# A scan and an ELU layer on one core: B and C of the later blocks turned by VectorE instead of TensorE, and the sums of the first layer's quarters joined

## The chip, the core and the metric

The kernel runs on one core of one Trainium2 chip. The metric is the device time of a whole execution in microseconds. The kernel before was run three times: 364.29, 364.76 and 364.16, median 364.29. One further execution was profiled; its span, from the first to the last instruction, is 362.9.

## The reference

There are two layers. The first is a chunked state-space scan over x (4 batches, 8 heads, 768 tokens, 32 wide) with decays a and with B and C (16 wide). The second takes the scan's output as 3072 tokens of 256 and computes ELU between two matrix products, 256 to 2048 and back.

```python
for c in range(nc):
    CB = np.einsum('bhin,bhjn->bhij', Cc, Bc)
    M = CB * L                                  # L: causal decays
    y_intra = np.einsum('bhij,bhjd->bhid', M, xc)
    y_inter = np.einsum('bhin,bhnd->bhid', Cc, state) * decay_to_i
    y[:, :, sl] = y_intra + y_inter
    state = decay_full * state + np.sum(Bx, axis=2)
h = x @ w_in
g = np.where(h > 0.0, h, np.exp(np.minimum(h, 0.0)) - 1.0)
out = g @ w_out
```

All of it is float32 (the weights come as 64-bit words that the kernel turns into float32 itself).

## The kernel before, in words

**Tiles.** The tokens are cut into 12 blocks of 256 (`NP`), all 8 heads in one. `place(n)` says which batch and which third a block is. A block has two halves of 128 tokens (`u`), and each of these two chunks of 64 (`v`).

**The scan of a block.** `load_bc` (line 106) brings B and C with the tokens on the partitions. `scaled` (line 359, on POOL) multiplies B by the decays. `turn` (line 368) brings B and C to the form with 8 heads x 16 states on the partitions: four TensorE transposes (line 374) into two PSUM tiles, a copy of B by ScalarE (line 378, `bt`), a masked C by VectorE (line 381, `ctm`). `turn_exp` (line 385) multiplies C by the decays `ec` (line 389, `cts`); `spread_exp` (line 340) fetches `ec` with one DMA per head. `scores` (line 450) multiplies masked C with B on TensorE, `weigh` (465) applies the decays, `sums` and `states` (480, 496) carry the state on, `across` and `inside` (522, 542) give the scan's output transposed in PSUM, which is copied to `yT`.

**The two matrix products.** Blocks 0 to 3 use plain products (`l1`, `l2`, lines 577 and 700) with ELU between them (`elu`, 598: exponential on ScalarE, then one VectorE instruction, line 605). From block 4 on, pairs of blocks n, n+1 are multiplied by a scheme with seven products where plain blocks take eight. For the first product each of 8 pieces i of a pair takes seven part products of 256 columns (line 655; each is two TensorE instructions in the profile) in two PSUM tiles c1 and c2 of one bank each. They are issued in three groups: `front` (three products, and a copy of the first by ScalarE, line 665), `mid` (two), `back` (two). Between them VectorE makes five sums of 256 columns: two in `front_sums` (673, 674), one in `mid` (682), two in `back` (689, 690). Then c1 and c2 go on the list `lag` and through ELU: `begin_elu` issues ScalarE's Relu (596), `elu` the rest. For the second product, `second(n)` (line 736) is a generator that gives out 56 small steps of products (line 759), with sums on VectorE and POOL (line 750, and `sub` at 723, `sum_t1` at 725, `sum_t2` at 729).

**The order of the work** is written out by hand: each engine does its instructions in the order in which the program issues them. The loop at line 1051 takes the pairs n = 4, 6, 8, 10, one stage each; a stage has 16 half steps k, two for each piece i = k // 2. An even half step does `front`, `front_sums`, the rest of an ELU, and four steps of the second product of the pair before (`l2s`). An odd one does `mid`, two steps, `back`, one step, the rest of an ELU and the start of the next. `scan_ahead` (967) puts the scan of the next pair between them: in stage n the loads and decays at k = 0 to 2, the turns at k = 5 and 7, `scores` at k = 9, and at i = 5 a version with `weigh`, `sums` and `states`. The stages n = 2 and n = 3 (line 1011) take single blocks.

**Buffers.** PSUM has 8 tiles of one bank: 7 in the pool `p_a`, given out in turn, and 1 in `p_o`. A new tile waits until the one seven before it has been read for the last time.

## Time and profile before

| engine | busy, us | share of the span | instructions |
|---|---|---|---|
| TensorE, matmuls (PE) | 354.3 | 98% | 3978 |
| TensorE, weight loads (PEld) | 316.9 | 87% | 3978 |
| VectorE (DVE) | 242.2 | 67% | 547 |
| ScalarE (ACT) | 200.7 | 55% | 499 |
| GpSimd (POOL) | 227.1 | 63% | 366 |

The matrix engine's clock is granted in full over the whole span, and the DMA engines are busy mostly in the first fifth. The costliest group of instructions is line 759 (the second product): 640 + 320 + 160 matmuls at 275 ns each. That is the time from the start of one to its end; they overlap, and in a stretch without waits one starts every 110 ns. Those of line 655 (256 columns) take 383 ns and start every 217 ns. VectorE's five sums per piece, of 32 pieces, are 13.5, 13.6, 13.8, 13.7 and 13.8 us. How to read a row of the timeline: start and length in us, engine, line, operation, output and inputs with shapes, and in brackets how long the engine had been idle before and what ended that.

### The profile page before, as it was taken

Reading aid. Unit: us, or ns where it says so; the run is one execution under the profiler, and the core shown is the slowest. Engines: PE = TensorE matmul, PEld = TensorE weight load, DVE = VectorE, ACT = ScalarE, POOL = GpSimd, SP = SyncE. Lnnn points to the kernel's source line nnn. Section 1 sums busy time; section 2 is a strip of 40 time slices with the busy share of each in tenths; the row PEclk is TensorE's granted clock in tenths of the full one; section 3 lists DMA queues with packets and bytes.
Section 4 is the critical chain, followed back from the end, with each engine's and each line's share of the span. In section 5 each row is a group of like instructions: output and inputs, shape, how many; then the busy total and the mean of one; then the engine's idle time right before and its main releaser. Section 6 shows DMA issues by size and latency. Waiting matters only on the chain.

```text
span 362.9 us, 10146 instructions
## 1 busy us (share of the span) xinstructions
PE 354.3 (98%) x3978; PEld 316.9 (87%) x3978; DVE 242.2 (67%) x547; ACT 200.7 (55%) x499; POOL 227.1 (63%) x366
## 2 busy tenths in 40 slices
PE   8899999999999999999999999999999999999996
PEld 5578778888888998898999998999989999999995
DVE  4989887972697668784567684666685666666212
ACT  4858969767435567635485735386735352534100
POOL 4454443663567896679457578567587555456893
PEclk9999999999999999999999999999999999999999
DMA  8877995563050560053530045540000100000001
GB/s 155 203 203 147 240 308 141 66 116 63 3 116 19 65 85 12 4 115 48 96 65 2 3 95 68 93 72 0 3 2 4 58 2 0 3 0 32 29 2 58
DMA packets 96239, 25.33 MB, mean 70 GB/s; under 512 B 77312, under 2 KB 92096, under 8 KB 96192
## 3 DMA queue, kind: packets, MB, share of 16 engines
q1 hardware_dynamic: 94016, 24.49, 33.0%
q8 instruction: 31, 0.51, 0.6%
q10 hardware_dynamic: 2176, 0.20, 0.4%
q14 instruction: 16, 0.13, 0.1%
HBM read 21.33 MB, written 3.34 MB: 68 GB/s over the span
## 4 chain that ended last, share of the span: by engine, by line
PE 81%; DVE 7%; ACT 3%; DMA 3%; SPq 2%; issue 2%; POOL 1%; ACTq 0%; DVEq 0%
PE ps_o L759 32%; PE ps_h L655 25%; PE ps_h L583 10%; PE ps_o L707 8%; SPq L112 2%; PE ps_g L459 1%; DMA w<-in_moe_w_in_dram 1%; DVE g L605 1%; PE ps_y L553 1%; ACT e L596 1%; PE ps_st L489 1%; ACT e L603 1%; DMA flat<-F 1%; DVE mag L183 1%; PE ps_y L534 1%
## 5 line engine op out<-in xcount | busy, mean ns | idle before, releaser
L596 ACT ACTIVATE e<-ps_h 128x512 f32<-128x512 f32 x96 | 56.5, 588 | 93.1 <-DVE ps_h L689 71.2
L605 DVE SCALAR_TENSOR_TENSOR g<-e,ps_h 128x512 f32<-128x512 f32 x96 | 65.3, 681 | 39.2 <-ACT e L603 35.8
L759 PEld LDWEIGHTS ps_o<-w_out,g 128*128 128x128 f32 x640 | 80.3, 192 | 3.3 <-issue 0.5
L759 PE MATMUL ps_o<-w_out,g 128*128 128x128 f32 x640 | 81.4, 275 | 0.0
L727 POOL TENSOR_TENSOR g<-g 128x256 f32<-128x256 f32 x34 | 24.8, 729 | 67.1 <-DVE g L605 67.1
L583 PE MATMUL ps_h<-yT,w_in 128*128 128x256 f32 x256 | 60.6, 383 | 2.5 <-POOL w_in L200 1.8
L603 ACT ACTIVATE e<-e 128x512 f32<-128x512 f32 x96 | 60.9, 634 | 2.2
L583 PEld LDWEIGHTS ps_h<-yT,w_in 128*128 128x128 f32 x256 | 47.8, 190 | 10.6 <-POOL w_in L200 2.8
L759 PE MATMUL ps_o<-w_sum,g 128*128 128x128 f32 x320 | 43.0, 275 | 0.0
L759 PEld LDWEIGHTS ps_o<-w_sum,g 128*128 128x128 f32 x320 | 41.1, 192 | 1.4
L439 ACT ACTIVATE L<-L,ncum 128x64 f32<-128x64 f32 x160 | 41.0, 338 | 0.0
L655 PE MATMUL ps_h<-y_sum,w_in 128*128 128x256 f32 x128 | 38.6, 383 | 0.7 <-DVE ps_h L682 0.7
L655 PE MATMUL ps_h<-y_sum,w_sum 128*128 128x256 f32 x128 | 38.5, 382 | 0.5 <-DVE g L605 0.5
L655 PE MATMUL ps_h<-yT,w_in 128*128 128x256 f32 x128 | 38.8, 385 | 0.0
L444 POOL TENSOR_SCALAR_AFFINE_SELECT L<-L 64x512 f32<-64x512 f32 x40 | 27.3, 682 | 13.1 <-ACT L L439 11.8
L707 PE MATMUL ps_o<-w_out,g 128*128 128x256 f32 x128 | 30.8, 383 | 0.0
L655 PEld LDWEIGHTS ps_h<-y_sum,w_sum 128*128 128x128 f32 x128 | 23.9, 190 | 5.3 <-DVE g L605 1.3
L723 POOL TENSOR_TENSOR g<-t,g 128x256 f32<-128x256 f32 x40 | 27.9, 729 | 0.8 <-PE ps_o L759 0.8
L723 POOL TENSOR_TENSOR t<-g 128x256 f32<-128x256 f32 x40 | 28.1, 736 | 0.2
L723 POOL TENSOR_TENSOR g<-g,t 128x256 f32<-128x256 f32 x40 | 27.9, 730 | 0.2
L707 PEld LDWEIGHTS ps_o<-w_out,g 128*128 128x128 f32 x128 | 23.7, 190 | 3.4 <-POOL L L444 0.2
L689 DVE TENSOR_TENSOR ps_h<-ps_h,u_sum 128x256 f32<-128x256 f32 x32 | 13.7, 429 | 18.3 <-PE ps_h L655 18.3
(109 smaller groups left out, 538.3 us busy)
## 6 DMA issues: line engine op xcount, KB each, us to landing
L<-flat SPq DMA_DIRECT2D x20, 256.0 KB, 5.3
w<-in_moe_w_in_dram SPq DMA_DIRECT2D x8, 512.0 KB, 5.2
w<-in_moe_w_out_dram SPq DMA_DIRECT2D x8, 512.0 KB, 6.1
xr<-in_x_dram SPq DMA_DIRECT2D x24, 128.0 KB, 3.4
out_dram<-c_sum SPq DMA_DIRECT2D x10, 256.0 KB, 2.1
bc<-in_B_dram SPq DMA_DIRECT2D x24, 64.0 KB, 4.4
bc<-in_C_dram SPq DMA_DIRECT2D x22, 64.0 KB, 3.4
ec<-flat_exp SPq DMA_DIRECT2D x72, 16.0 KB, 1.7
```

The costliest lines, as they stand in the source:

```text
L439: nc.scalar.activation(L[:, h, u], L[:, h, u], ACT.Exp, bias=ncum[:, u, row:row + 1])
L444: nc.gpsimd.affine_select(out=part, in_=part, pattern=[[0, 4], [0, 2], [1, Q]], compare_op=ALU.is_ge, fill=0.0, base=0, channel_multiplier=-1)
L583: nc.tensor.matmul(out=ps[:, j], lhsT=w_in[:, k, m * P:(m + 1) * P], rhs=yT[n // 2][:, k, n % 2].rearrange("p u i -> p (u i)"), start=(k = ...
L596: nc.scalar.activation(begun[0], lag[0][2], ACT.Relu, scale=-1.0)
L603: nc.scalar.activation(e, e, ACT.Exp, scale=-1.0)
L605: nc.vector.scalar_tensor_tensor(out=g_of[n, i], in0=e, scalar=1.0, in1=ps, op0=ALU.subtract, op1=ALU.max)
L655: nc.tensor.matmul(out=out, lhsT=lhsT, rhs=rhs, start=first, stop=True, skip_group_check=True)
L689: nc.vector.tensor_tensor(out=c1[:, 1], in0=c1[:, 1], in1=u[:, 0], op=ALU.add)
L707: nc.tensor.matmul(out=o_of[n][:, ts], lhsT=g_of[n, j][:, m % 2, ts * P:(ts + 1) * P], rhs=w_out[:, m], start=(m == 0 and ts == 0), stop=( ...
L723: nc.gpsimd.tensor_tensor(out=out, in0=in0, in1=in1, op=ALU.subtract)
L727: eng.tensor_tensor(out=b12, in0=b12, in1=g_of[n, i][:, 0], op=ALU.subtract)
L759: nc.tensor.matmul(out=ps[:, ts], lhsT=b[:, ts * P:(ts + 1) * P], rhs=a[:, i], start=(i == chunk[0] and ts == 0), stop=(i == chunk[-1]), s ...
```

## The change

From block 6 on B and C no longer pass through TensorE and PSUM. `load_bc` fetches B twice: once with the tokens on the partitions, for `scaled`, and B and C once more in an order (4 heads x 32 groups of 8 tokens on the partitions) in which VectorE's transposes of 32x32 squares give the wanted form. `turn_square` issues one such VectorE instruction for B and one for C; `mask_heads` and `turn_exp` follow, now from SBUF. `turn_step` deals these four parts of two blocks out over the odd half steps 1, 3, 5, 7 of a stage, an early place between `mid` and `back` and a late one after `back`; block 6's first three come in stage n = 3. The loads are issued half a stage sooner. `spread_exp` becomes one DMA.

In the first product the part products change their places: c2 takes the two that `front` leaves open and both of `back`, c1 those of `mid`'s sum. `front_sums` is then one sum over both halves of c2, `mid` has one of 256 columns, and `back` one over both halves of c2. c1 is complete after `mid` and goes on the list there. Because the quarters lie elsewhere, `second` finds them through `quarters`. In the loop `begin_elu` now follows `mid`, and `next_elu`, `begin_elu` follow `back` ahead of the one step; at i = 5 the steps are 4, 1, 2 for 3, 2, 2. In the beginning `w_sum(0)` is done in quarters. Some pools have fewer buffers (`sc`, `cts`, `ob`), and `bt` becomes a tile for B and C.

```diff
@@ load_bc
+        if n > 5:
+            st[n]["b"] = raw.tile([P, 2, NH, N], F32, tag="b", name="b_tok", bufs=2)
+            for u in range(2):
...
+                nc.sync.dma_start(
+                    out=st[n]["b"][:, u], in_=B[b, :, sl, :].rearrange("h s n -> s h n"))
...
+            for k, src in enumerate((B, C)):
+                for m in range(2):
+                    nc.sync.dma_start(
+                        out=squares[:, k, m],
+                        in_=src[b, m:NH:2, g * BLK:(g + 1) * BLK, :].rearrange(
+                            "q (c t) n -> q c (t n)", t=8))
+            return
@@ spread_exp
-        for h in range(NH):
-            row = rows_of(n).start + NG * h
-            nc.sync.dma_start(
-                out=ec[N * h:N * (h + 1)].rearrange("n u i -> n (u i)"),
-                in_=flat_exp[row:row + 1].to_broadcast([N, BLK]))
+        nc.sync.dma_start(
+            out=ec.rearrange("p u i -> p (u i)"),
+            in_=flat_exp[rows_of(n)].unsqueeze(1).to_broadcast([NH, N, BLK]))
@@ after turn
+    def turn_square(n, k):
...
+        nc.vector.transpose(
+            out=s["squares"][:, k].rearrange("p u i -> p (u i)").rearrange("p (c t) -> p t c", t=8),
+            in_=s["bc"].rearrange("p k u h n -> p k (u h n)").rearrange(
+                "p k (m t n) -> p k t m n", m=2, n=N)[:, k])
...
+    def turn_part(n, part):
+        if part < 2:
+            turn_square(n, 1 - part)
+        elif part == 2:
+            mask_heads(n)
+        else:
+            turn_exp(n)
@@ front, front_sums, mid, back
-        copy = conv.tile([P, BLK], F32, tag="sgn", name="p_copy")
-        nc.scalar.copy(out=copy, in_=c1[:, 0])
-        part_product(c2[:, 1], s_in[0][:, i], t[:, 1], True)
-        part_product(c2[:, 0], a21[:, i], t[:, 0])
+        u = conv.tile([P, 3, BLK], F32, tag="mag", name="u_sum")
+        nc.scalar.copy(out=u[:, 0], in_=c1[:, 0])
+        part_product(c2[:, 0], s_in[0][:, i], t[:, 1], True)
+        part_product(c2[:, 1], a21[:, i], t[:, 0])
...
-        nc.vector.tensor_tensor(out=u[:, 0], in0=c2[:, 1], in1=copy, op=ALU.add)
-        nc.vector.tensor_tensor(out=u[:, 1], in0=c2[:, 0], in1=u[:, 0], op=ALU.add)
+        nc.vector.tensor_tensor(
+            out=u[:, 1:3], in0=c2, in1=u[:, 0].unsqueeze(1).to_broadcast([P, 2, BLK]), op=ALU.add)
...
-        part_product(c1[:, 1], s_in[1][:, i], y_sums[n][:, 2])
-        nc.vector.tensor_tensor(out=c2[:, 1], in0=c1[:, 1], in1=u[:, 1], op=ALU.add)
+        part_product(c2[:, 0], s_in[1][:, i], y_sums[n][:, 2])
+        nc.vector.tensor_tensor(out=c1[:, 1], in0=c2[:, 0], in1=u[:, 2], op=ALU.add)
+        lag.append((n, i, c1))
...
-        part_product(c1[:, 1], a22[:, i], y_sums[n][:, 3])
-        part_product(c2[:, 0], s_in[2][:, i], b22)
-        nc.vector.tensor_tensor(out=c1[:, 1], in0=c1[:, 1], in1=u[:, 0], op=ALU.add)
-        nc.vector.tensor_tensor(out=c2[:, 0], in0=c2[:, 0], in1=u[:, 0], op=ALU.add)
-        lag.append((n, i, c1))
+        part_product(c2[:, 0], a22[:, i], y_sums[n][:, 3])
+        part_product(c2[:, 1], s_in[2][:, i], b22)
+        nc.vector.tensor_tensor(out=c2, in0=c2, in1=u[:, 0:2], op=ALU.add)
         lag.append((n + 1, i, c2))
@@ scan_ahead
-                load_bc(m + i)
+                if m == 4:
+                    load_bc(m + i)
...
-            if i in (5, 7):
+            if m == 4 and i in (5, 7):
...
+        if n % 2 == 1 and i in (1, 3) and n + 3 + i // 2 < NP:
+            load_bc(n + 3 + i // 2)
+        if n == 3 and i > 3 and i < 7:
+            turn_part(6, i - 4)
@@ after scan_ahead
+    def turn_step(n, k, late):
...
+        if m == 6:
+            steps = [(7, 0), (7, 1), (7, 2), (6, 3)]
+            if not late:
+                turn_part(*steps[k // 2])
+            elif k == 7:
+                turn_part(7, 3)
+        else:
+            at = k // 2 * 2 + late
+            turn_part(*[(m, 0), (m, 1), (m, 2), (m + 1, 0), (m + 1, 1), (m + 1, 2), (m, 3), (m + 1, 3)][at])
@@ the loop over pairs, odd half steps
                 mid(n, i)
...
+                begin_elu()
+                turn_step(n, k, False)
                 l2s(2)
                 back(n, i)
-
+                next_elu()
+                begin_elu()
+                turn_step(n, k, True)
...
                 l2s(1)
-                next_elu()
-                begin_elu()
```

## The prediction

> **What bounds the kernel now.** I read the page's first part first, then the busy time of the engines by stretches, then the chain of work that ended last, then single stretches of the timeline.

> ```profile
> PE 354.3 (98%) x3978; PEld 316.9 (87%) x3978; DVE 242.2 (67%) x547; ACT 200.7 (55%) x499; POOL 227.1 (63%) x366
> ...
> 110.00:167.00 57.00, 56.33 (x813) 51.47 (x815) 40.85 (x99) 31.25 (x82) 45.00 (x75) 1.00 0.34 53
> 167.00:224.00 57.00, 56.54 (x700) 51.73 (x684) 37.88 (x89) 33.43 (x88) 39.19 (x63) 1.00 0.32 54
> 224.00:277.00 53.00, 52.95 (x636) 49.04 (x637) 34.94 (x81) 32.16 (x86) 35.03 (x56) 1.00 0.17 30
> ```

> The stretches read: window, its length, then PE, PEld, DVE, ACT, POOL busy with counts. From 44 us on the chain of work is the matrix engine almost without a break, so time is saved by taking PE work out or PE waits out, and by nothing else. DVE is free for about a third of each stretch. The PE work that the change removes is in these rows (the line's own answer, and the chain in order of time with start, length, what):

> ```profile
> L374 PE MATMUL ps_tb<-ident,bc x24: 272/273/327, 6.7 to 254.9; 128*128 128x128 f32 x24
> L374 PE MATMUL ps_tc<-ident,bc x24: 272/273/273, 6.9 to 255.1; 128*128 128x128 f32 x24
> ```
> ```profile
> 139.07 0.68 DVE ctm L381
> 139.76 0.33 DVE cts L389
> 140.09 0.34 DVE u_sum L673
> 140.43 0.02 issue
> 140.45 0.42 DVE u_sum L674
> 140.88 0.06 DVE g L605
> 140.94 0.45 issue
> 141.39 0.42 DVE c_sum L750
> 141.80 0.35 DVE ps_h L682
> 142.16 0.04 issue
> 142.20 1.13 PE ps_h L655 x4
> 143.33 0.44 PE ps_o L759 x4
> 143.77 0.22 PE ps_tb L374 x2
> 143.99 0.22 PE ps_tc L374 x2
> ```

> A turn is four PE instructions, two times 0.22 us: 0.44 us per block. The 273 ns of one is latency, overlapped with the next. The same stretch shows the largest PE stall: from 139 to 142 us the chain leaves PE and runs through DVE, where mask (ctm), scaling (cts) and sums stand in one queue ahead of L682. The other stalls of this phase are at the first front of stages six and eight:

> ```profile
> 168.16 0.30 PEld L655 LDWEIGHTS ps_h<-y_sum,w_sum 128*128 128x128 f32 x2 [0.60 <-DVE g L605]
> 223.82 0.30 PEld L655 LDWEIGHTS ps_h<-y_sum,w_sum 128*128 128x128 f32 x2 [0.67 <-DVE g L605]
> ```

> There a PSUM tile is not free until ELU of the pair before has been done. Measured from start to start of the matmuls (217 ns apart when nothing waits), PE loses at these places: 0.15 + 0.83 us at 139 to 142, 0.36 at 168, 0.43 at 224, and 0.10 more on the first matmul after a wait, seven times: 2.5 us in all.

> [...] L674 with 256 takes 424 ns, L605 with 512 takes 681.

> **The change part by part.**

> *Turns on DVE.* Blocks 6 to 11 lose 4 PE transposes each: 6 x 0.44 = **2.64 us off PE**, all on the path. They also lose an ACT copy (358 ns) and two PSUM tiles each. DVE gains 12 squares of 128x256. Unknown; nearest price 424 ns[...]. I take 0.42. The mask then reads SBUF where it read PSUM (682 ns; taken the same), and the scaling 0.41 as before. Per stage DVE gains 4 x 0.42 = 1.7 us. It hides in the gaps shown here (start, length, instruction, idle before):

> ```profile
> 237.00 0.69 DVE L605 SCALAR_TENSOR_TENSOR g<-e,ps_h 128x512 f32<-128x512 f32 x1 [0.89 <-ACT e L603]
> ...
> 240.06 0.43 DVE L682 TENSOR_TENSOR ps_h<-ps_h,u_sum 128x256 f32<-128x256 f32 x1 [0.51 <-PE ps_h L655]
> ...
> 241.39 0.43 DVE L689 TENSOR_TENSOR ps_h<-ps_h,u_sum 128x256 f32<-128x256 f32 x1 [0.89 <-PE ps_h L655]
> ```

> The early piece stands between L682's sum and the joined last sum, where DVE waits 0.89 us for PE; because the joined sum waits for both quarters (0.43 more) the gap is 1.3 us. The late piece stands behind ELU's subtraction and ahead of the joined front sum.

> *Joined sums.* Five DVE sums of 421 to 430 ns (2.13 us) become one of 512, one of 256, one of 512: 0.69 + 0.43 + 0.69 = 1.81. 32 x 0.32 = 10 us off DVE, more than the 12 x 0.42 = 5 us of squares. On PE: nothing directly. One wait is new: the middle's second product (c2[0]) now waits for the joined front sum. Behind it on PE stand the two second-product steps, the back and everything after. In before I compared the end of L674 with the start of that product: DVE is ahead by 0.80 us in 13 of 32 pieces, by 0.1 to 0.6 in the rest but five; the joined sum ends 0.15 earlier than L674. Of those five one is the place at 139 to 142 that loses its cause, three are level within 0.03 (first piece of stages six and eight, last piece of the last), one has 2.8. So new waits: about 0, taken in the next paragraph for the stage heads.

> *Order of ELU.* c1 is whole after the middle, so ACT's Relu starts half a step earlier and c1's PSUM tile comes free earlier. At 164 to 168 us in before, Relu waited until 166.12 for two back sums that stood behind a c_sum waiting for POOL; now it starts about 1.5 us sooner, more than the 0.36 and 0.43 lost there. But the copy of P1 there stands behind six yT copies on ACT (168 to 170): joined sum no sooner than 170.08 + 0.37 + 0.69 = 171.14 if ACT is not earlier, and PE, 0.47 sooner, wants it at 170.87. So of some 0.6 us at each head (0.36 or 0.43, and two refills) I count 0.35, as ACT is partly earlier. **0.7 us.** At 139 to 142 the mask, one scaling, the bt copies and the PSUM tiles leave; of 1.18 us I count **1.1**. The last 0.10 (332.67) I leave.

> *Stage three.* Two squares and a mask (1.5 us) are added to DVE at steps 4 to 6, where it also makes weight sums. DVE is idle 3.25 us before 118.90, and the tiles behind are needed two steps later: nothing.

> *DMA.* load_bc of blocks 6 to 11 goes from 4 issues to 6 (about 0.6 us each on SP) and moves one half stage forward, past spread_cum and the loads of x. SP is idle there (no issue from 135 to 156 us), and the buffer it waits for is read last by POOL's scaled (88.83 to 90.06 in stage three). spread_exp goes from 8 issues (3.8 to 5.5 us of SP) to one. Its readers come ten us later: nothing.

> *First weight piece.* w_sum in halves: two POOL adds of about 0.49 us for one of 0.84. The first l1 can start 0.3 earlier, DVE beside it may slow. That phase ends on DMA landings (the chain goes flat, SP, w until 35.14): 0, with 0.3 either way.

> **Sum.** 2.64 + 1.1 + 0.7 = 4.4 us off the span of 362.9: 358.5. The runs are 364.16 to 364.76, median 364.29, some 1.4 above the profiled span; taken off the median: **359.9**.

> **Rivals.**

> 1. *Only the transposes pay.* The waits come back at the new place, the middle behind the joined sum, because ACT's copy and POOL's c_sum set DVE's times and not DVE's own load. For it: the three level pieces, and DVE c_sum waits for POOL (10.5 us in 6 waits). Against: 27 pieces with slack. 364.3 - 2.6 = 361.7, with half of it given back 363.0. If new waits eat all 2.6, 364.3: no change.

> 2. *Slower: a square is too long for its gap.* The late piece has 0.42 us plus the rest to the middle's product: joined sum at 237.46 to 238.15 against 239.43 in the stretch shown, 1.2 us. So PE waits once late squares pass 1.6 us, or an early one 1.3. In stages six and eight k=1 holds two squares, k=3 one late, k=5 one early. At 2.6 us each PE loses 1.3 + 2.2 - 1.2 = 2.3 at k=1, 1.0 at k=3, 0.4 at k=5: 3.6 a stage, 7.2 in all, 364.3 - 4.4 + 7.2 = 367.1. Even at about 2.2 us. For it: 32-byte steps on the output, on which the trace is silent.[...]

> 3. *More is gained.* All 2.5 us of waits and 0.3 at the start: 364.3 - 2.6 - 2.5 - 0.3 = 358.9, or 358.2 if the first pieces after the scores also flow better.

> **Numbers.** Forecast (359.2 to 361) 0.57; only the transposes (361 to 363.3) 0.20; more gained (below 359.2) 0.10; no change 0.04; slower 0.09. A measurement of this kernel tells 0.2%, 0.73 us, from no change. Faster by that 0.87, same 0.04, slower 0.09. The range 358.4 to 363.2 leaves out the slower and no-change cases and the edge of the third.

> **What would show it.** Right: L374 with 24 PE matmuls instead of 48; DVE squares near 0.42 us; front and last sums near 0.69; no PE stall over 0.3 us at the place of 139 to 142; PE busy time down 2.6 us with the span. Wrong: L655's weight loads waiting for the front sums in many pieces; squares over 1.3 us; c_sum on DVE waiting longer for POOL than 10.5 us; or a start that ends later than 44 us. What would upset the whole: a PE order that is no longer gapless because ACT, not DVE, ends last at each stage's head.

## The result, and the profile after

The changed kernel takes 363.01 us in the median of 9 runs (360.79 to 364.12), beside 365.23 us (9 runs) for the kernel before. The ratio is 0.9945, 95% interval 0.9924 to 0.9966: **2.0 us faster** (1.2 to 2.8; the two medians lie 2.2 apart), where 4.4 us were forecast. A second series of 22 runs gave 0.9952 (0.9932 to 0.9972). The profiled span is 362.1 us; before it was 362.9.

The page's busy times and its row of granted clock, kernel after:

```profile
PE 352.8 (97%) x3954; PEld 315.5 (87%) x3954; DVE 240.4 (66%) x495; ACT 200.8 (55%) x493; POOL 232.0 (64%) x368
...
PEclk9999999999999999999999999999998999999999
```

PE has 24 matmuls less, but only 1.5 us less busy time, and its share fell from 98% to 97%. The new thing is the single 8 in the clock row: slice 31 of 40, 271.6 to 280.6 us. Windows around it, kernel after (window, its length, busy of PE, PEld, DVE, ACT, POOL with counts, clock, DMA share, GB/s):

```profile
255.00:267.00 12.00, 12.00 (x178) 10.55 (x177) 8.60 (x22) 6.16 (x16) 9.52 (x16) 1.00 0.01 1
267.00:269.00 2.00, 1.99 (x103) 1.67 (x102) 1.90 (x5) 0.56 (x2) 0.98 (x4) 1.00 0.03 8
269.00:271.30 2.30, 0.48 (x46) 0.32 (x25) 0.15 (x1) 0.37 (x1) 2.22 (x4) 1.00 0.00 0
271.30:275.50 4.20, 4.20 (x84) 3.77 (x84) 0.00 (x0) 1.84 (x5) 3.00 (x5) 0.59 0.01 4
275.50:285.00 9.50, 9.50 (x65) 8.91 (x64) 5.86 (x12) 4.35 (x9) 4.46 (x7) 1.00 0.09 29
```

In the third window PE works 0.48 of 2.30 us, and DVE, ACT and DMA are next to idle as well. Only POOL is busy (2.22 us), with sums of the second product, and the trace shows no wait of PE for it. In the fourth the clock is 0.59. The timeline of PE's matmuls there, after and then before (start, length, instruction, count, idle before):

```profile
267.52 1.24 PE L576 MATMUL ps_y<-cts,Sx 32*64 32x64 f32 x64
268.69 0.79 PE L595 MATMUL ps_y<-M,xr 64*32 64x64 f32 x56
271.30 1.07 PE L595 MATMUL ps_y<-M,xr 64*32 64x64 f32 x72 [1.81 <-issue]
272.30 2.07 PE L807 MATMUL ps_o<-w_sum,g 128*128 128x128 f32 x8
274.17 1.06 PE L697 MATMUL ps_h<-yT,w_in 128*128 128x256 f32 x2
```
```profile
272.28 0.91 PE L534 MATMUL ps_y<-cts,Sx 32*64 32x64 f32 x64
273.12 1.51 PE L553 MATMUL ps_y<-M,xr 64*32 64x64 f32 x128
274.56 1.16 PE L759 MATMUL ps_o<-w_sum,g 128*128 128x128 f32 x8
```

This is the last call of `across` and `inside`, 192 small products back to back; I call such a stretch a **dense part**. Before, the 128 products of `inside` run in 1.51 us. After, PE stops in their middle, after 56, and the view names no releaser ("issue"). From 272.0 to 275.4 us matmuls are then twice as far apart, 427 ns instead of 217 at 256 columns: eight of L807 take 2.07 us instead of 1.16. In the trace's record the clock is one half for 3.41 us there, from 0.7 us after the end of a standstill of 2.0 us (start to start, 269.27 to 271.30 us).

To see what the rest of the change brought, I cut each profiled span at the first product of the first dense part and of the last one (in the timeline, the first L576; L534 before):

```
kernel        to first dense   first to last dense   last dense to end   span
before             111.57            160.72                90.62         362.9
turns_only         110.58            158.21                90.90         359.7
sums_only          112.02            159.44                90.74         362.2
after              110.92            156.60                94.58         362.1
after_again        111.99            156.77                94.14         362.9
```

The middle column holds the turns and most of the sums, and there the change takes off 160.72 - 156.60 = **4.1 us** (4.0 in the second profile), close to the 4.4 of the forecast. Then 94.58 - 90.62 = **4.0 us** are given back (3.5 in the second), in a stretch where only the joined sums are new, and `sums_only` takes 90.74 there. In the median of all runs the loss is less: both profiled executions had a mean granted clock of 0.993, while 21 of the change's 31 runs had 0.998 or more (and 18 of 49 runs of the kernel before had 0.995 or less, so a stretch at half clock is nothing new).

### The profile page after: what moved, and what is told of

Its sections match the earlier page's. It is cut to its first block, busy times and chain, and to the rows that moved or that the text cites. A ratio compares the mean times of both kernels' runs of the same rounds, so it can differ in the third digit from the quotient of the medians.

```text
span 362.1 us, 9921 instructions
## 1 busy us (share of the span) xinstructions
PE 352.8 (97%) x3954; PEld 315.5 (87%) x3954; DVE 240.4 (66%) x495; ACT 200.8 (55%) x493; POOL 232.0 (64%) x368
## 4 chain that ended last, share of the span: by engine, by line
PE 88%; POOL 5%; DVE 4%; issue 1%; ACT 1%; POOLq 0%; DVEq 0%
PE ps_o L807 32%; PE ps_h L697 25%; PE ps_h L625 14%; PE ps_o L746 8%; PE ps_y L595 2%; PE ps_g L501 2%; POOL g L762 2%; PE ps_y L576 1%; PE ps_st L531 1%; PE ps_idle L232 1%; POOL g L774 1%; DVE mag L207 1%; DVE mag L200 1%; POOL w_sum L673 1%; DVE M L510 1%
## 5 line engine op out<-in xcount | busy, mean ns | idle before, releaser
L807 PEld LDWEIGHTS ps_o<-w_out,g 128*128 128x128 f32 x640 | 80.3, 192 | 3.3 <-issue 0.5
L807 PE MATMUL ps_o<-w_out,g 128*128 128x128 f32 x640 | 81.4, 275 | 0.0
L807 PE MATMUL ps_o<-w_sum,g 128*128 128x128 f32 x320 | 43.9, 279 | 0.0
L807 PEld LDWEIGHTS ps_o<-w_sum,g 128*128 128x128 f32 x320 | 41.9, 195 | 1.5 <-PE ps_y L595 0.2
L730 DVE TENSOR_TENSOR ps_h<-ps_h,u_sum 128x512 f32<-128x512 f32 x32 | 22.3, 698 | 23.6 <-PE ps_h L697 23.5
L486 POOL TENSOR_SCALAR_AFFINE_SELECT L<-L 64x512 f32<-64x512 f32 x40 | 28.1, 702 | 13.0 <-ACT L L481 11.7
L722 DVE TENSOR_TENSOR ps_h<-ps_h,u_sum 128x256 f32<-128x256 f32 x32 | 13.8, 431 | 30.5 <-PE ps_h L697 30.1
L714 DVE TENSOR_TENSOR u_sum<-ps_h,u_sum 128x512 f32<-128x512 f32 x32 | 22.0, 687 | 13.3 <-PE ps_h L697 8.0
L762 POOL TENSOR_TENSOR t<-g 128x256 f32<-128x256 f32 x40 | 29.4, 767 | 0.3
L762 POOL TENSOR_TENSOR g<-g,t 128x256 f32<-128x256 f32 x40 | 28.7, 750 | 0.3
```

The source lines that it names most:

```text
L486: nc.gpsimd.affine_select(out=part, in_=part, pattern=[[0, 4], [0, 2], [1, Q]], compare_op=ALU.is_ge, fill=0.0, base=0, channel_multiplier=-1)
L730: nc.vector.tensor_tensor(out=c2, in0=c2, in1=u[:, 0:2], op=ALU.add)
L762: nc.gpsimd.tensor_tensor(out=out, in0=in0, in1=in1, op=ALU.subtract)
L807: nc.tensor.matmul(out=ps[:, ts], lhsT=b[:, ts * P:(ts + 1) * P], rhs=a[:, i], start=(i == chunk[0] and ts == 0), stop=(i == chunk[-1]), s ...
```

## The experiments

Two theories. **L** (supply of instructions): the trace has a DMA queue that carries instructions. It brings PE's in blocks of 16 KB, 31 of them in a run. The traces hold 8056 instructions of PE before and 8011 after (matmuls, weight loads and some hundred others), so a block is about 256 of them; the places of the standstills will show the number. Where one block ends and the next begins I call a **border**. A dense part of 384 instructions in 2.4 us eats such a block faster than the queue, which needs about 2.4 us from the start of a fetch to the first use (268.93 to 271.30 us in the profile after), can bring the next. In the profile after, PE has done 64 + 64 loads and matmuls of L576 and 57 + 56 of L595 when it stops: it is at a border, 241 instructions into the dense part. Before, the border lay 194 in. **W**, the rival: the missing time went into new waits for DVE, whose squares are longer than forecast and whose joined sum `mid` now waits for, and the standstill costs the median nothing.

### The change again, and its two halves

`turns_only` has VectorE's squares, loads and `turn_step`, but the sums, quarters and order of ELU of before. `sums_only` has the joined sums and the early Relu, but all blocks turned by TensorE:

```diff
 turns_only
-        u = conv.tile([P, 3, BLK], F32, tag="mag", name="u_sum")
-        nc.scalar.copy(out=u[:, 0], in_=c1[:, 0])
+        copy = conv.tile([P, BLK], F32, tag="sgn", name="p_copy")
+        nc.scalar.copy(out=copy, in_=c1[:, 0])
...
 sums_only
-        if n > 5:
+        if n > 99:
...
-            if m == 4 and i in (5, 7):
+            if i in (5, 7):
```

> The changed kernel once more. Theory L (one late fetch of PE's instructions): in the profiled execution PE stood still for 2.0 us in the dense products of the scan (269.3 to 271.3) because a block of its instructions came 5.7 us after it was due instead of about 1, and the half clock that followed cost some 1.5 more; the late fetch is chance, so a second profile shows none or another place, a span of 358 to 359.5 and PE waits on the front sums of about 1.4 us as before. Theory W (waits): the waits on sums and copies took the gain back; then the span is again near 362 with the clock at 1.0. Theory A (alignment): the standstill is at the same instruction again, span near 362.

> B and C turned by DVE as in the change, but the first product's sums, quarters and ELU order as before. Prediction's term: 24 PE transposes gone, 2.64 us, the places after stage heads keep their waits (1.2 us). Theory L: PE's instructions as in the changed kernel, 362.0 to 363.0 where before is 365.2, ratio 0.991 to 0.994. Theory W: the squares, at 0.64 us each, and masks at 0.93 add 9 us to DVE and nothing is taken off, so PE waits more than in before; ratio 0.995 to 1.0.

> The joined sums and the earlier Relu of the change, with the turns left on PE as before. Prediction's term: stage heads lose their PSUM waits (about 1.2 us in two), new waits on the joined front sum about 0.5; ratio 0.997 to 0.999, PE matmuls 3978. Theory W: the new waits in the middle outweigh it, ratio 1.0 to 1.003.

`after_again`: 363.07 us, ratio 0.9952 (0.9932 to 0.9972), and in its profile the same standstill at the same instruction (1.7 us). The expectation under L, that the place is chance, was wrong. `turns_only`: 362.33 us, 0.9933 (0.9911 to 0.9954). `sums_only`: 363.98 us, 0.9972 (0.9956 to 0.9987). By the ratios the halves are worth 2.4 us (1.7 to 3.2) and 1.0 us (0.5 to 1.6), 3.4 together; whole, the change is worth 1.8 to 2.0. So the halves are sound, and something seems lost when they come together. Neither half has a standstill in its profile. In `turns_only` (timeline of PE):

```profile
268.80 0.91 PE L576 MATMUL ps_y<-cts,Sx 32*64 32x64 f32 x64
269.64 1.51 PE L595 MATMUL ps_y<-M,xr 64*32 64x64 f32 x128
```

### Moving the dense parts against the borders

`pad160` adds 40 idle products of 16 columns (160 PE instructions) ahead of the first l1. The first border then falls 41 to 84 instructions into each of the four dense parts, and the next, 256 later, still within it, so that two blocks are used up in one dense part. `pad24` adds 24 in the same place (6 products).

```diff
+    for _ in range(40):
+        nc.tensor.matmul(
+            out=ps_idle[0:32, 0, 0:16], lhsT=idle[0:32, 0:32], rhs=idle[0:32, 0:16],
+            start=True, stop=True, tile_position=(0, 0), skip_group_check=True)
     l1(0, 0)
```

> The changed kernel with 40 tiny products (160 PE instructions in the stream) in a gap of the start where PE waits 1.3 us anyway. Nothing else moves, but the borders of the 256-instruction blocks that PE fetches move through the program. Theory L: then blocks lie wholly in the dense products of four scans (384 instructions in 2.3 us), each is used up in about 1.8 us while a fetch takes about 3.4 from its trigger; PE stands still about 1.6 us at each of four places, 6 us slower than the changed kernel, perhaps with half clock behind them. Theory W: no difference over 0.3 us.

> The changed kernel with 24 extra PE instructions in the gap at the start: the border at the standstill moves 24 instructions away from the dense part, about 2 us more time for the late fetch. Theory L: standstill in stage 8 gone or under 0.5 us, none elsewhere; 1 to 1.5 us less than the changed kernel, ratio 0.990 to 0.993. Otherwise equal to the changed kernel.

`pad160`: 379.77 us, ratio 1.0417 (1.0382 to 1.0452). PE now stands still in all four dense parts; three of them in its timeline:

```profile
121.69 0.66 PE L595 MATMUL ps_y<-M,xr 64*32 64x64 f32 x42 [2.00 <-issue]
...
178.60 0.42 PE L595 MATMUL ps_y<-M,xr 64*32 64x64 f32 x22 [2.58 <-issue]
...
235.26 0.80 PE L595 MATMUL ps_y<-M,xr 64*32 64x64 f32 x44 [2.33 <-issue]
```

Counted from PE's first instruction in the trace, it stops after 3009, 4289, 5569 and 6849 instructions, and in the changed kernel after 6593. All these numbers leave 193 when divided by 256, and so do those of all 14 standstills in dense parts, in the nine profiles that have any: PE stops at a border, and a block is 256 instructions. Three of the four standstills here are followed by 3.4 us at half clock; the longest, at 178.6 us, isn't. The size of the loss (17 us, where 6 were expected) isn't clean, since PE also stops among the tiny products at the start, after 449 instructions (193 and 256), and is at half clock for 10.2 us there (mean granted clock of that execution 0.972, with 10.2 us more behind the three standstills). That the standstills come and go with the number of instructions ahead of them is clear. `pad24`: 362.75 us, 0.9944 (0.9924 to 0.9963), no gain in the median, although its profile has no standstill in a dense part and a span of 358.9 us. It too stops at the start, after 449 instructions. Of its 19 runs 15 had a granted clock of 0.995 or less (median 363.2 us), the other four took 360.3 to 361.9. That the half clock lies at the start, as in `pad160`, is likely but not shown. The next pair is free of this.

### 24 instructions ahead of the last dense part, or behind it

`pad24s8` gives six score products of block eleven twice, at step 9 of stage n = 8, ahead of the last dense part; `late24` puts six products of 16 columns at that stage's last front, behind it.

```diff
 pad24s8, in scores
+                        if n == 11 and u == 1 and q < 3:
+                            nc.tensor.matmul(
+                                out=gs[q][toks, at, u], lhsT=s["bt"][rows, u, toks],
+                                rhs=s["ctm"][rows, u, :, toks], start=True, stop=True,
+                                tile_position=(32 * q, Q * v), skip_group_check=True)
 late24, in front
+        for _ in range(6 if (n, i) == (8, 7) else 0):
+            part_product(
+                c1[:, 0, 0:16], a11[:, i],
+                yT[n // 2][:, 0, 0].rearrange("p u i -> p (u i)")[:, 0:16], True)
```

> The changed kernel with six of the score products of blocks ten and eleven given twice (24 more TensorE instructions at step 9 of the stage that begins at 224 us, some 1.3 us of work at most; the output is the same). Theory L (the standstill in the last dense part of the scan is a late fetch of TensorE's instructions, and where it falls hangs on the number of instructions ahead of it): the 24 instructions move the dense part from 241 to 217 instructions ahead of the block border, the standstill of 2.0 us at 269 us and the 3.4 us at half clock after it go away or shrink below 0.7 us; profiled span 358.8 to 360.0, median 361.0 to 361.9, ratio 0.989 to 0.992, and few runs with a clock below 0.997. Against it (the standstill comes from what the products read or write, or it costs the median nothing): standstill unchanged, median 363.0 to 363.6.

> The changed kernel with six small products of 16 columns (24 TensorE instructions, about 1 us at most) at the last front of the stage that begins at 224 us, which is behind the last dense part; each is overwritten by the product after it, the output is the same. Theory L: nothing moves ahead of the dense part, the standstill of 1.5 to 2 us at 269 us and the half clock after it stay; median 363.0 to 364.0, some of the runs with a clock below 0.997. Against it (24 more instructions anywhere help, as a rest or a change of rhythm would): median near 361.4 as with the 24 ahead of the dense part.

`pad24s8`: **361.43 us**, ratio 0.9913 (0.9884 to 0.9942). `late24`: 363.67 us, 0.9976 (0.9961 to 0.9990). The two intervals don't meet. The medians overstate what the place is worth, since the six products of `late24` themselves take some 1.3 us in its trace and those of `pad24s8` some 0.4. The standstills are the better evidence. Timelines of PE, first `pad24s8`, then `late24`:

```profile
268.59 1.24 PE L581 MATMUL ps_y<-cts,Sx 32*64 32x64 f32 x64
269.76 1.51 PE L600 MATMUL ps_y<-M,xr 64*32 64x64 f32 x128
271.20 1.16 PE L812 MATMUL ps_o<-w_sum,g 128*128 128x128 f32 x8
```
```profile
267.11 1.24 PE L576 MATMUL ps_y<-cts,Sx 32*64 32x64 f32 x64
268.28 0.79 PE L595 MATMUL ps_y<-M,xr 64*32 64x64 f32 x56
270.33 0.96 PE L595 MATMUL ps_y<-M,xr 64*32 64x64 f32 x72 [1.26 <-issue]
271.22 1.16 PE L811 MATMUL ps_o<-w_sum,g 128*128 128x128 f32 x8
```

With the 24 ahead, all 128 products are in one piece; with the 24 behind, PE stops after 56, as in the changed kernel. `late24` also shows that the half clock doesn't follow every standstill: L807's like (L811) takes 1.16 us here. That fits the median, which loses less (361.43 to 363.0, 1.6 us; 1.4 by the ratios, 1.3 either way) than the first two profiles did (4.0 and 3.5). `pad24s8` is 3.2 us faster than before by its ratio (2.1 to 4.2), about what the halves add up to (3.4), and has the lowest median of all kernels tried. Its interval still overlaps the changed kernel's at the edge.

The queue can be seen at work. The DMA view from 262.0 to 268.5 us, after and then `pad24s8`:

```profile
DMA packets 0, 0.00 MB, mean 0 GB/s; under 512 B 0, under 2 KB 0, under 8 KB 0
```
```profile
DMA packets 1, 0.02 MB, mean 3 GB/s; under 512 B 0, under 2 KB 0, under 8 KB 0
...
q8 instruction: 1, 0.02, 0.9%
```

In one the block comes ahead of the dense part; in the other nothing has been fetched when it begins, though the queues are empty.

### Is it W?

`squares_twice` issues each DVE square twice. `split_front` gives the joined front sum as two of 256 columns, in the order in which the products need them; `split_pad24s8` has this and the 24 instructions of `pad24s8`.

```diff
 squares_twice
+        for _ in range(2):
           nc.vector.transpose(
 split_front
-        nc.vector.tensor_tensor(
-            out=u[:, 1:3], in0=c2, in1=u[:, 0].unsqueeze(1).to_broadcast([P, 2, BLK]), op=ALU.add)
+        for r in range(2):
+            nc.vector.tensor_tensor(out=u[:, 1 + r], in0=c2[:, r], in1=u[:, 0], op=ALU.add)
```

> The changed kernel with each of the 12 square transposes on DVE done twice (12 x 0.64 us more on DVE, the same result). The prediction's step that DVE's gaps hide the squares up to 1.3 us early and 1.6 us late: no change over 0.5 us. Theory W (DVE's load sets the new waits on the front sums): PE waits on L714 rise from 1.4 us by 0.6 for each late square and each that shifts a c_sum, 3 to 7 us slower, ratio 1.003 to 1.015.

> The changed kernel with the front's joined sum of 512 columns given as two of 256, in the order that the next products need them. If the joined front sum is what mid's second product waits for (1.36 us of TensorE's waits with the refills after them): the first sum ends some 0.26 us earlier, the waits at 138.5, 154, 208 and 262 us fall to 0.4 to 0.6 us in all, and DVE has 16 x 0.17 us more work that nothing waits for; median 362.1 to 362.7 with the standstill at 269 us left as it is. If those waits are hidden by others: 362.9 to 363.3. If DVE's longer work counts: above 363.3.

> Both edits: six score products twice and the front's sum in two. Theory L and the front's wait, added: profiled span 357.8 to 359.5, median 360.2 to 361.3, ratio 0.986 to 0.990, below both kernels. If the standstill moves back because the front's earlier end lets TensorE reach the dense part sooner: 362.0 to 363.0.

`squares_twice`: 362.44 us, 0.9944 (0.9924 to 0.9964), level with the change. Its squares, by form (busy, mean ns):

```profile
L414 DVE STREAM_TRANSPOSE bct<-bc 128x256 f32<-128x256 f32 x24 | 15.5, 645 | 0.4
```

7.8 us more on DVE cost nothing: the squares are hidden, and W falls for them. Its other part, the wait for the joined sum, is real; its size (1.4 us) is worked out below. `split_front`: 363.52 us, 0.9957 (0.9941 to 0.9972), a miss; its profile has the standstill too. The waits didn't shrink; the product is released only by the second of the two sums, and two small ones end later than one large (0.74 us for both, 0.69 for L714 in after; timeline of `split_front`):

```profile
139.13 0.74 DVE L715 TENSOR_TENSOR u_sum<-ps_h,u_sum 128x256 f32<-128x256 f32 x2
...
139.93 0.70 PE L697 MATMUL ps_h<-y_sum,w_sum 128*128 128x256 f32 x2 [0.63 <-DVE u_sum L715]
```

So `split_pad24s8` (362.38 us, 0.9930, 0.9902 to 0.9957) is no better than `pad24s8`.

### Breaking the dense part up

`break4` puts four steps of the second product between `across` and `inside`, so that PE has 1.7 us of large products in the middle of a dense part; `pad160_break` does so in `pad160`.

```diff
-            inside(across(*ns), *ns)
+            y = across(*ns)
+            if more:
+                more(4)
+            inside(y, *ns)
```

> The version with 160 extra PE instructions (379.8 us), and in stages 4, 6 and 8 four steps of the second product (1.8 us of slow PE instructions) between across and inside, so that no block of 256 PE instructions is used up in under about 3.5 us there. Theory L (fetch of PE's instructions): the standstills of 2.8, 2.5 and 2.1 us in these stages go, with the half clock behind them; the one of 2.2 us before stage 4 stays, as does what the padding costs at the start: 9 to 11 us less than with the padding alone, 369 to 371. If the standstills had another cause (waits of the scan itself): less than 2 us gained.

> The changed kernel with four steps of the second product between across and inside in stages 4, 6, 8, no padding. Theory L: the standstill of 1.7 to 2.0 us in stage 8 and the half clock behind it go; two more switches of PE's tile form per stage cost 0.25 each (0.75 in all); median 1 to 2 us under the changed kernel, ratio to before 0.990 to 0.993, and fewer runs with a granted clock under 0.997. Theory W (waits): no gain, or 0.7 slower.

`pad160_break`: 374.59 us, 1.0295 (1.0262 to 1.0329), beside 1.0417 unbroken, but not the 369 to 371 us expected. Its standstills are shorter (0.88 us where there were 2.58), and no half clock follows them:

```profile
119.59 0.66 PE L595 MATMUL ps_y<-M,xr 64*32 64x64 f32 x42 [1.51 <-issue]
...
175.00 0.64 PE L595 MATMUL ps_y<-M,xr 64*32 64x64 f32 x38 [0.88 <-issue]
```

`break4`: 363.66 us, 0.9974 (0.9962 to 0.9985). Its fetch starts as late as in the changed kernel (5.4 us in the measure of the next part), but the standstill is gone (largest gap 0.42 us), and none of its 22 runs had a granted clock under 0.997. The 0.25 us put down for the switches of tile form was an estimate: in before 205 ns pass from start to start between L759's last product and L534's first, and 146 between L553's last and L759's first, against 110 between two of L759. Still no time is won: the four steps are missing as a filler elsewhere, and PE waits for `mid`'s sum, near 172, 227 and 283 us; the first of these:

```profile
171.84 0.70 PE L697 MATMUL ps_h<-y_sum,w_in 128*128 128x256 f32 x2 [0.53 <-DVE ps_h L722]
```

### Why is the fetch late?

I call the number of instructions from the start of the last dense part to the next border its **place**. The 31 fetches of the changed kernel, taken in order as those of its 31 borders, start 1.2 us (median) after PE has come to 297 instructions ahead of their border, 21 of them within 2 us; I take that as the **asking place** (it is inferred, not seen); with the 2.4 us to the first use that makes 3.6, where the 3.4 in the expectation of `pad160` was an estimate. Late ones aren't rare: seven in the first 105 us start 3.2 to 5.3 us after it. The one of the standstill starts 5.7 us after it. `turns_only` has almost the same place (244) and no late fetch, so the place alone can't be all. `before208` puts 208 more instructions (52 repeated score products) into the kernel before, to bring its dense part to the same place. There the repeats of one product stand one behind the other; `before208_even` gives them in whole passes, and `sums204_even` does so, with 204, in `sums_only`.

```diff
 before208
+                        for _ in range((7 if v == 0 else 6) if n == 11 and u else 0):
+                            nc.tensor.matmul(
...
 before208_even, sums204_even (51 for 52)
+            for r, u, v, q in [
+                    (r, u, v, q) for r in range(5 if n == 11 else 1)
+                    for u in range(2) for v in range(2) for q in range(4)]:
+                if r == 4 and 8 * u + 4 * v + q >= 4:
+                    continue
```

> The kernel before the change, with 52 of the score products of blocks ten and eleven given again (208 more TensorE instructions at step 9 of the stage that begins at 224 us; the output is the same). They move its last dense part from 194 to 242 instructions ahead of a block border, where the changed kernel has 241. If the place against the border alone makes the standstill: TensorE stands still some 2 us in the last inside products (about 273 to 277 us) and runs 3.4 us at half clock after it, on top of the 2 to 3 us that the 208 instructions cost[...]: span 367 to 369, many runs over 367.5. If something else of the change (its earlier loads, its DVE squares, its order of ELU) makes the late fetch: no standstill, only the 2 to 3 us of work, 366.5 to 367.5 with clock 1.0.

> The kernel before the change, with 208 more TensorE instructions at step 9 of the stage that begins at 224 us as in before208, but given as whole passes over the score products of block eleven, so that they run side by side in the array and cost 3 to 5 us instead of 15 (the output is the same). The last dense part lies 242 instructions ahead of a block border, as in the changed kernel (241). If the place alone makes the standstill: 1.5 us or more in the last inside products, fetch over 4.5 us after its trigger. If the place is not enough, as before208 had it: no standstill, fetch about 2 us after its trigger, span 366 to 368.

> The joined sums and early Relu with TensorE's turns (sums_only), and 204 more TensorE instructions in the same way, which bring its last dense part to 242 ahead of a border. If the order of the joined sums together with the place makes the late fetch: standstill of 1.5 to 2 us in the last inside products, fetch about 5 us after its trigger, some 1.5 us longer than before208_even less 1.0 us for the sums. If it takes the DVE squares or the changed loads as well: no standstill, fetch about 2 us after its trigger, about 1 us shorter than before208_even.

`before208` was badly made: 382.02 us, 1.0494 (1.0456 to 1.0533). In its trace the repeats take some 15 us in place of the 2 to 3 expected, one behind the other (13 of them in 1.42 us) and from 268.6 us on at half clock. It had no standstill. The even ones overlap (43 in 0.89 us in `before208_even`) and cost little: `before208_even` 366.56 us, 1.0052 (1.0017 to 1.0088); `sums204_even` 366.37 us, 1.0057 (1.0034 to 1.0081). Level, where the sums alone had been worth 1.0 us; with intervals of 0.9 and 1.3 us either way the times alone wouldn't show it. Timelines of PE, first `before208_even`, then `sums204_even`:

```profile
273.94 0.91 PE L536 MATMUL ps_y<-cts,Sx 32*64 32x64 f32 x64
274.79 1.51 PE L555 MATMUL ps_y<-M,xr 64*32 64x64 f32 x128
```
```profile
272.34 1.24 PE L578 MATMUL ps_y<-cts,Sx 32*64 32x64 f32 x64
273.51 0.79 PE L597 MATMUL ps_y<-M,xr 64*32 64x64 f32 x57
275.57 0.96 PE L597 MATMUL ps_y<-M,xr 64*32 64x64 f32 x71 [1.27 <-issue]
```

By these profiles, one of each kernel, the standstill needs the place and the joined sums' order; DVE's squares and the new loads of B and C aren't needed. In both late kernels the product at the asking place is the one that waits for the joined front sum. The last run takes that wait away:

```diff
-                l2s(1)
+                l2s(2)
                 mid(n, i)
                 begin_elu()
                 states(m)
-                l2s(2)
+                l2s(1)
                 back(n, i)
```

> The changed kernel with one step of the second product moved, at i = 5 of each stage, from behind mid to ahead of it (2, 1 steps for 1, 2). Nothing is added or left out, and the last dense part stays at 241 ahead of a border. The product that waits for the joined front sum (0.14 us at 154, 208 and 262 us; at 262.6 it is the very instruction at which the fetch should be asked for) then comes 0.9 us later and finds the sum done. If the wait at the asking place makes the fetch late: fetch 1 to 3 us after its trigger, no standstill, span 358.8 to 360.2, median 360.8 to 361.8, ratio 0.988 to 0.991, below both kernels. If something else of the order does: fetch still about 5 us late, standstill 1.5 to 2 us, only 0.5 us gained by the three waits, median 362.4 to 363.0.

`step_ahead`: 363.46 us, 0.9945 (0.9916 to 0.9974). The standstill stays (timeline), and a wait comes up at `back` instead:

```profile
265.60 0.70 PE L697 MATMUL ps_h<-y_sum,w_in 128*128 128x256 f32 x2
...
272.10 0.96 PE L595 MATMUL ps_y<-M,xr 64*32 64x64 f32 x72 [1.30 <-issue]
```

So a wait just at the asking place isn't the cause. What in the joined sums' order holds the fetch back **stays open**. The traces add one thing: in the late cases (over 5 us) the fetch starts 1.7 to 2.3 us after PE has passed the border before, in the others 1.5 us before to 0.3 us after that. The runs together (place of the last dense part, in instructions; start of the fetch after the asking place, largest gap from start to start in the dense part, last dense part to the end, in us):

```
kernel            place   fetch   gap    to end
before             194    2.06    0.15   90.62
sums_only          190    1.36    0.23   90.74
turns_only         244    1.81    0.15   90.90
before208_even     242    2.05    0.15   90.66
pad24s8            217    3.20    0.23   90.91
split_pad24s8      217    3.35    0.23   90.90
pad24              220    3.56    0.23   90.88
after              241    5.66    2.03   94.58
after_again        241    5.06    1.72   94.14
squares_twice      241    5.11    1.49   92.44
step_ahead         241    5.80    1.51   92.46
split_front        241    5.04    1.70   94.00
late24             241    5.12    1.48   93.79 (24 more in it)
sums204_even       242    5.11    1.48   92.26
```

From place 241 or 242 the dense part begins 4.25 us after the asking place (4.9 in `step_ahead`), from 217 6.7 us after: there a fetch that starts 3.2 us after it still comes in time, here one of 5 us doesn't. PE takes 1.75 us for the 241 instructions (267.52 to 269.27 us in after), so the block should be there 4.25 + 1.75 = 6.0 us after the asking place. With 2.4 us to the first use it comes after 5.1 + 2.4 = 7.5: a standstill of 1.5 us, as in `squares_twice`, `late24` and `sums204_even`.

## Why the prediction was half right

*Turns.* Forecast 2.64 us off PE; `turns_only` is 2.4 us faster by its ratio and 2.5 in the middle column. The transposes of blocks 0 to 5 remain, as expected: 12 matmuls each for B and C. Right.

*Squares and mask.* In after (by tile; minimum, median, maximum in ns, first and last start):

```profile
L413 DVE STREAM_TRANSPOSE bct<-bc x12: 633/638/642, 109.3 to 242.7; 128x256 f32<-128x256 f32 x12
L421 DVE TENSOR_TENSOR ctm<-bct,hmask x6: 689/961/1210, 116.7 to 245.3; 128x512 f32<-128x512 f32 x6
```

A square takes 0.64 us, not the 0.42 I chose; the trace of before has no transpose on DVE, and 0.42 was an estimate from the 424 ns of L674, a sum of 256 columns. The mask took up to 1.21 where 0.68 was taken over from PSUM. Both sizes were wrong and neither mattered, as the gaps were wide enough: rival 2 is refuted, by `squares_twice` too. (Its sum has slips that change nothing: 2.3 + 1.0 + 0.4 is 3.7, and by its own limit of 1.3 us an early square of 2.6 us loses 1.3, not 0.4.)

*Joined sums.* 0.69, 0.43, 0.70 us (L714, L722, L730): right. "New waits about 0" was wrong. `mid`'s second product waits for the joined front sum (matrix engine's weight loads, us in total, times, longest; then the chain of after at 139 us):

```profile
PEld ps_h L697 <- DVE u_sum L714: 2.2, 5, 0.9
```
```profile
138.61 0.69 DVE u_sum L714
139.30 0.04 issue
139.35 0.70 PE ps_h L697 x2
```

On PE this is 0.63 us at 138.5 and 0.14 each at 154, 208 and 262, with a refill of 0.10 behind each: 1.4 us. The three small ones lie at i = 5, where the change moves one step of the second product from behind `front` to ahead of it. The prediction left out that this brings `mid`'s product closer to the sum: it starts 1.23 us after `front`'s last product, the wait included, where it was 1.54. And its sign "no PE stall over 0.3 us at the place of 139 to 142" failed.

*Order of ELU and the place at 139 to 142.* Of the 1.18 us there 0.73 came back as this new wait, so it gave 0.45, not 1.1. The stage heads gave 1.0, more than the 0.7 counted: the 0.36 at 168 and the 0.43 at 224 are gone, with two refills. The two misses nearly cancel, which is luck. In the middle column the sums alone give 1.3 us and the whole change 4.1, so the waits gave 4.1 - 2.5 = 1.6 in place of 1.8.

*Stage three, DMA, first weight piece.* Taken as 0. That DVE may slow beside POOL's add is seen in before: L190 on 256 columns took 0.42 us at 11.40, with POOL idle, and 0.83 at 12.27, with POOL at an add of L200 for 0.56 of it. The first dense part begins between 110.4 and 112.0 us in the profiles of the change and its kin, at 111.6 before: no effect to be seen.

*The sum.* **This is the step that failed.** "2.64 + 1.1 + 0.7 = 4.4 us off the span" held up to the last dense part (4.1 of 4.4 in the profile) and lacks a term: what fewer PE instructions do to the place of later ones against the borders of the fetched blocks. The prediction put the supply of PE's instructions at nothing without a word. It gave back 3.5 to 4.0 us in the two profiles and about 1.4 in the median (3.4 from the halves, 3.2 by the ratio of `pad24s8`, 1.8 to 2.0 measured). The rest, 3.4 in the medians against 4.4, is not explained; the halves are known to 0.6 and 0.8 us only. The forecast of 359.9 us also stood on a base of 364.29 us, three runs; that of nine is 365.23, which makes 0.9 of the 3.1 us by which it missed. Rival 1's "half of it given back" had the time, 363.0, by luck: the new waits (1.4 us) were made up for by the old ones that went, and the standstill took the time. The share of PE in the chain of work, on which the whole was built, says only that time lies on PE, not that PE is supplied.

## What to carry to other kernels

Taking instructions off the bounding engine also shifts all that follow it: if a long run of tiny products stands later in the program, look in the profile after for a gap that nobody releases ("issue") inside it (here 2.0 us), and for half clock behind it (here 3.4 us), before blaming the edit. Cut the span at landmarks and compare the stretches one by one; here that shows at once that the edited stretch gave 4 us and an unedited one took them back. A gap of this kind can be moved by some two dozen harmless instructions ahead of it, at a gain of about 1.5 us here, but such a remedy is tied to this very program and has to be measured after every edit.
